# One set of order rules for the scheduler of an attention kernel, and small layer-norm steps moved to VectorE

## The chip, the cores and the metric

The kernel runs on one core of a Trainium2 chip. The metric is the device time of one execution in microseconds (us). Before the change it is 709.93 us, the median of three runs (709.76 to 710.06). The profiled execution shows a span of 708.0 us from the first to the last instruction.

## The reference, cut to what matters

A token block of 2048 rows and 640 columns is normalised; attention with 32 query heads of width 20 and one shared key and value head is added to a squared-ReLU feed-forward layer and to the input.

```python
xn = _layernorm(x)                                   # (x - mean) / sqrt(var + 1e-5)
q = (xn @ wq) -> 32 heads of 20;  k = xn @ wk;  v = xn @ wv
p = softmax((q @ k.T) * 20 ** -0.5)                  # 32 x 2048 x 2048
attention = (p @ v) -> (2048, 640) @ wo
h = relu(xn @ w1 + b1) ** 2                          # 2048 x 1536
return x + attention + (h @ w2 + b2)
```

The score matrix has 134 million elements. It is worked off in tiles of 128 keys by 512 queries: 4 query chunks x 8 groups of 4 heads make 32 blocks, and each block has 16 key tiles x 4 heads, so there are 2048 tiles in all. The four heads of one key tile are called a set when VectorE takes them.

## The kernel before

Two paths make the exponential of a score tile. ScalarE takes two or three tiles at a time from PSUM and writes exp to `PT`. VectorE and GpSimd take whole sets: VectorE turns each score into a 16-bit pattern whose bits, read as bf16, are a rough power of two; three more passes add a constant to the pattern (a quarter step each), on whichever of VectorE and GpSimd the scheduler expects to be done first; and four weighted value matmuls add the four approximations up.

```python
# a score step for ScalarE: 2 or 3 tiles, in as many PSUM banks
return Op(f"ACT{st_['j']}", "ACT", 0.05 + 0.4267 * n, [lambda e: e.activation(
    out=PT[:, s0:s0 + n, :], in_=ps[:, b0:b0 + (n - 1) * db + 1:db, :], func=AF.Exp, bias=-EXP_SHIFT, scale=SCALE)], deps)
# ... a tile for VectorE (tbuf lies in tmore or in x_sb)
d1 = op(f"D1_{n}_{i}", "DVE", 0.60, lambda e: e.tensor_scalar(
    out=L[:, cs].bitcast(U16), in0=ps[:, bank, :], scalar1=XA, scalar2=XB, op0=ALU.mult, op1=ALU.add), ...)
# ... and the three pattern passes of a full set
tp = max(free["POOL"] - now, 0.0) + sum(o.dur for o in pool_q) + 1.86
td = max(free["DVE"] - now, 0.0) + sum(o.dur for o in dve_q) + 0.6
eng = "POOL" if tp <= td + par("PBIAS") else "DVE"
```

TensorE makes the scores with four heads side by side on groups of 32 rows (one burst, called mode R in the code), and everything else (values, projections, feed-forward, output) in groups of four matmuls of 32 columns (mode C).

The order of the instructions on every engine is laid out before the launch by a list scheduler in the kernel's own Python. It keeps a clock for each engine, with durations written beside each operation, and always takes the ready operation that can start first; among those that could start within `EPS` the one with the lowest priority number. Some twenty parameters set those choices. They are read by `par`, and the kernel before overrides them anew for each stretch of 10 us of the scheduler's clock:

```python
STG = 10.0
RULES = {1: {'PVA': 0.95, 'EPS': 0.2, 'DGAP': 0.8},
         2: {'JIT': 0.9},
# ... some 55 rows cut
         69: {'R3': 0, 'WARM': 0.78, 'NOPEN': 1, 'URG': 2, 'D1P': 0.5, 'ND': 2, 'MPRIO': 0.9, 'DQP': 0.95, 'PBIAS': 1}}

def next_stage():
    while free["ACT"] >= stage[0] * STG:
        stage[0] += 1
        # ...
        now_rules.clear()
        now_rules.update(RULES.get(stage[0], {}))

def par(name):
    return now_rules.get(name, DEFAULTS[name])
```

A few of the parameters: `R3` sets how many PSUM banks must be free before three tiles rather than two go into one ScalarE step (at least 3 + R3); `NOPEN` is the number of VectorE sets that may be open at once; `DRATE` and `DLAST` decide until when a set is still taken from the current block; `PBIAS` favours GpSimd for a pattern pass; `MPRIO`, `PVA`, `DQP` are priorities of TensorE's work; `WARM` is the share of TensorE's time below which it puts in filler matmuls on zeros.

```python
banks = None
if len(ok) >= 3 + par("R3"):          # ok: banks that are free in time
    ap = [(a, a + d, a + 2 * d) for d in (1,) for a in range(NB - 2 * d) if {a, a + d, a + 2 * d} <= set(ok)]
    if ap:
        banks = list(ap[0])
if banks is None:
    can = sorted((max(st_of[bk], st_of[bk + 1], t0), bk) for bk in range(NB - 1) if ...)
    banks = [can[0][1], can[0][1] + 1]
```

Of the kernel before, what the change touches and what calls it, by code (L numbers as in the profile page):

```python
# [9 lines left out]
ALU = mybir.AluOpType  # L10
# [15 lines left out]
EPS = 1e-5  # L26
# [9 lines left out]
def _pl(z):  # L36
# [16 lines left out]
EVP = 0.8  # L53
JIT = 0.8
R3 = 2
NOPEN = 2
# [3 lines left out]
DRATE = 0.95  # L60
DLAST = 7.5
# [17 lines left out]
ACTEV = (0, 2)  # L79
KEEP = 1  # L80
DJIT = 9.0
RULES = {1: {'PVA': 0.95, 'EPS': 0.2, 'DGAP': 0.8},
         2: {'JIT': 0.9},
         3: {'JIT': 0.9, 'R3': 0},
         5: {'EPS': 0.2, 'DJIT': 0.6},
         6: {'SQP': 2, 'EPS': 0.06},
         7: {'SQP': 2, 'EPS': 0.06},
         8: {'DQP': 0.95, 'D1P': 1},
         9: {'MPRIO': 1.0},
         10: {'DRATE': 1.1, 'D1P': 1},  # L90
         12: {'R3': 2, 'ND': 1, 'JIT': 1.0, 'MPRIO': 1.1},
         13: {'NOPEN': 1, 'DRATE': 1.1},
         14: {'NOPEN': 1, 'DRATE': 1.1, 'KEEP': 2, 'DLAST': 3.5},
         15: {'R3': 1},
         16: {'R3': 1, 'DJIT': 1.0, 'ND': 3, 'DRATE': 0.8, 'DGAP': 0.25},
         17: {'R3': 1, 'DJIT': 1.0, 'ND': 3, 'DRATE': 0.8, 'DGAP': 0.25},
         18: {'PP': 0.9, 'NOPEN': 1},
         19: {'PP': 0.9, 'NOPEN': 1, 'EVP': 2, 'SQP': 1.5, 'DJIT': 9},
         20: {'PP': 4, 'NOPEN': 1, 'EVP': 2, 'SQP': 1.5, 'DJIT': 9},
         21: {'EVP': 2, 'URG': 2},  # L100
         22: {'JIT': 0.82},
         23: {'IDLE': 0.2, 'D1P': 3},
         24: {'IDLE': 0.2, 'D1P': 3, 'PBIAS': 1.5, 'DRATE': 0.95},
         25: {'DJIT': 0.6, 'DRATE': 0.95, 'URG': 4},
         26: {'D1P': 1, 'PVA': 2.1, 'DGAP': 0, 'DRATE': 0.95},
         27: {'JIT': 1.0, 'SQP': 0.7},
         28: {'EPS': 0.06, 'IDLE': 0.5},
         29: {'PP': 0.9, 'DRATE': 0.95, 'DLAST': 4.5},
         30: {'NOPEN': 3, 'DQP': 2.05, 'EPS': 0.12},
         38: {'DQP': 2.05, 'PBIAS': 2.5},  # L110
         39: {'DQP': 2.05, 'PBIAS': 2.5, 'PP': 2.5, 'IDLE': 0.1, 'ND': 1, 'DRATE': 1.1},
         40: {'DLAST': 2.5, 'R3': 1, 'EPS': 0.06, 'EVP': 0.3},
         41: {'DLAST': 2.5, 'R3': 1, 'EPS': 0.03, 'EVP': 0.3, 'DJIT': 0.3},
         42: {'DLAST': 2.5, 'R3': 1, 'EPS': 0.03, 'EVP': 0.3, 'DJIT': 0.3, 'PBIAS': 0.3},
         43: {'IDLE': 2, 'DJIT': 9, 'DLAST': 2.5, 'DRATE': 0.95},
         44: {'IDLE': 2, 'DJIT': 9, 'DLAST': 2.5, 'DRATE': 0.95, 'EPS': 0.12},
         45: {'IDLE': 2, 'DJIT': 9, 'DLAST': 2.5, 'DRATE': 0.95, 'EPS': 0.12, 'SQP': 0.7, 'BEHIND': -0.3, 'KEEP': 1},
         46: {'DGAP': 1.5, 'MPRIO': 1.1, 'BEHIND': 0.5},
         47: {'DGAP': 1.5, 'MPRIO': 0.5, 'BEHIND': 0.5, 'PBIAS': 0.3, 'R3': 1, 'NOPEN': 2},
         48: {'DGAP': 1.5, 'MPRIO': 0.5, 'BEHIND': 0.5, 'PBIAS': 0.3, 'R3': 1, 'NOPEN': 2, 'D1P': 0.5, 'DRATE': 1.1},  # L120
         49: {'DGAP': 1.5, 'MPRIO': 0.9, 'BEHIND': 0.5, 'PBIAS': 0.3, 'R3': 1, 'NOPEN': 2, 'D1P': 3, 'DRATE': 1.1, 'DLAST': 3.5, 'EVP': 2},
         50: {'DGAP': 1.5, 'MPRIO': 0.9, 'BEHIND': 0.5, 'PBIAS': 0.3, 'R3': 1, 'NOPEN': 2, 'D1P': 3, 'DRATE': 1.1, 'DLAST': 3.5, 'EVP': 2},
         51: {'DGAP': 1.5, 'MPRIO': 0.9, 'BEHIND': 0.5, 'PBIAS': 0.3, 'R3': 1, 'NOPEN': 2, 'D1P': 3, 'DRATE': 1.1, 'DLAST': 3.5, 'EVP': 2, 'EPS': 0.06, 'PP': 4},
         52: {'DGAP': 1.5, 'MPRIO': 0.9, 'BEHIND': 0.5, 'PBIAS': 2.5, 'R3': 1, 'NOPEN': 2, 'D1P': 1, 'DRATE': 1.1, 'DLAST': 3.5, 'EVP': 2, 'EPS': 0.06, 'PP': 4, 'SQP': 0.7, 'URG': 4},
         53: {'DGAP': 1.5, 'MPRIO': 0.9, 'BEHIND': 0.5, 'PBIAS': 2.5, 'R3': 1, 'NOPEN': 2, 'D1P': 1, 'DRATE': 1.1, 'DLAST': 3.5, 'EVP': 1.1, 'EPS': 0.06, 'PP': 2.5, 'SQP': 0.7, 'URG': 4},
         54: {'DGAP': 1.5, 'MPRIO': 0.9, 'BEHIND': 0.5, 'PBIAS': 2.5, 'R3': 1, 'NOPEN': 2, 'D1P': 1, 'DRATE': 1.1, 'DLAST': 3.5, 'EVP': 1.1, 'EPS': 0.06, 'PP': 2.5, 'SQP': 0.7, 'URG': 6, 'KEEP': 3},
         55: {'DGAP': 1.5, 'MPRIO': 0.9, 'BEHIND': 0.5, 'PBIAS': 2.5, 'R3': 1, 'NOPEN': 2, 'D1P': 1, 'DRATE': 1.1, 'DLAST': 3.5, 'EVP': 1.1, 'EPS': 0.06, 'PP': 2.5, 'SQP': 0.7, 'URG': 6, 'KEEP': 3},
         56: {'JIT': 0.82, 'MPRIO': 0.9, 'PP': 2.5},
         57: {'JIT': 0.82, 'MPRIO': 0.9, 'PP': 2.5, 'WARM': 0.85, 'R3': 1, 'SQP': 0.7},
         58: {'JIT': 0.82, 'MPRIO': 0.9, 'PP': 2.5, 'WARM': 0.85, 'R3': 1, 'SQP': 0.7},  # L130
         59: {'DLAST': 4.5},
         60: {'DLAST': 4.5, 'NOPEN': 2, 'MPRIO': 1.0},
         61: {'DLAST': 4.5, 'NOPEN': 2, 'MPRIO': 1.0},
         62: {'R3': 0, 'WARM': 0.78},
         63: {'R3': 0, 'WARM': 0.78, 'NOPEN': 1, 'URG': 2},
         64: {'R3': 0, 'WARM': 0.78, 'NOPEN': 1, 'URG': 2},
         65: {'R3': 0, 'WARM': 0.78, 'NOPEN': 1, 'URG': 2},
         66: {'R3': 0, 'WARM': 0.78, 'NOPEN': 1, 'URG': 2, 'D1P': 1, 'ND': 2, 'MPRIO': 0.9, 'DQP': 0.95},
         67: {'R3': 9, 'WARM': 0.78, 'NOPEN': 1, 'URG': 2, 'D1P': 1, 'ND': 2, 'MPRIO': 0.9, 'DQP': 0.95},
         68: {'R3': 9, 'WARM': 0.78, 'NOPEN': 1, 'URG': 2, 'D1P': 0.5, 'ND': 2, 'MPRIO': 0.9, 'DQP': 0.95, 'PBIAS': 1},  # L140
         69: {'R3': 0, 'WARM': 0.78, 'NOPEN': 1, 'URG': 2, 'D1P': 0.5, 'ND': 2, 'MPRIO': 0.9, 'DQP': 0.95, 'PBIAS': 1}}
HOOK = None
PRIO = {'XN1': 0.13}
NBEF = {'S4a': 6.0, 'AG5': 10.23, 'PW1': 4.94}
# [90 lines left out]
def bass_parallel_sum__grouped_kv_mqa__dense_activation_squared_relu__prompt_kernel(nc, A_x, A_wq, A_wk, A_wv, A_wo, B_x, B_w1, B_b1, B_w2, B_b2, out):  # L235
    es = ExitStack()
    with es:
# [118 lines left out]
        def op(name, eng, dur, fn, deps=(), **kw):  # L356
            o = Op(name, eng, dur, [fn], deps, **kw)
            o.prio = PRIO.get(name, o.prio)
            o.nb = NBEF.get(name, 0.0)
            ev = [d for d in o.deps if isinstance(d, str)]  # L360
            if ev:
                late.setdefault(ev[0], []).append(o)
            else:
                QUE[eng].append(o)
            return o
# [59 lines left out]
        def rows(st):  # L425

            p = ROWP[st // 4]
            small, pp = (("DVE", 0.08), p - 0.1) if st < 4 else (("POOL", 0.13), st // 4 - 0.5)
            if st in ACTST:
                k = ACTST.index(st)  # L430
                jk = OC[:, 0, :, :].rearrange("p c n -> p (c n)")[:, k * D:(k + 1) * D] if k < 4 else out_sb[:, k - 4, :]
                s1 = op(f"S{st}a", "ACT", 0.72, lambda e: e.activation(out=jk, in_=x_sb[:, st, :], func=AF.Identity, scale=-1.0 / D, accum_out=mv[:, st, 0:1]), [x_op[st]], lat=0.2)
                ag = op(f"S{st}b", "ACT", 0.9, lambda e: e.activation(out=jk, in_=x_sb[:, st, :], func=AF.Square, bias=mv[:, st, 0:1], accum_out=mv[:, st, 1:2]), [s1], lat=0.25)
                ve = op(f"VE{st}", "DVE", 0.08, lambda e: e.tensor_scalar(out=mv[:, st, 1:2], in0=mv[:, st, 1:2], scalar1=1.0 / D, scalar2=EPS, op0=ALU.mult, op1=ALU.add), [ag], prio=p - 0.1)
                opm = ALU.add
            else:
                s1 = op(f"S{st}a", "DVE", 0.40, lambda e: e.bn_stats(out=stats6[:, st, 0, :], in_=x_sb[:, st, 0:320]), [x_op[st]], prio=p)  # L437
                s2 = op(f"S{st}b", "DVE", 0.40, lambda e: e.bn_stats(out=stats6[:, st, 1, :], in_=x_sb[:, st, 320:640]), [x_op[st]], prio=p)  # L438
                ag = op(f"AG{st}", "DVE", 0.19, lambda e: e.bn_aggr(out=mv[:, st, :], in_=stats6[:, st, :, :].rearrange("p a b -> p (a b)")), [s1, s2], prio=p - 0.1)
                ve = op(f"VE{st}", *small, lambda e: e.tensor_scalar(out=mv[:, st, 1:2], in0=mv[:, st, 1:2], scalar1=EPS, scalar2=None, op0=ALU.add), [ag], prio=pp)  # L440
                opm = ALU.subtract
                if st in POOLXN:
                    s1 = op(f"NM{st}", *small, lambda e: e.tensor_scalar(out=mv[:, st, 0:1], in0=mv[:, st, 0:1], scalar1=-1.0, scalar2=None, op0=ALU.mult), [ag], prio=pp)
                    opm = ALU.add
            pw = op(f"PW{st}", "POOL", 0.52, lambda e: e.tensor_tensor(out=rstd[:, st:st + 1], in0=mv[:, st, 1:2], in1=nhalf[:, 0:1], op=ALU.pow), [ve, c_half], lock=True, prio=st // 4)  # L445
            eng, dur = ("POOL", 0.87) if st in POOLXN else ("DVE", 0.36)
# [579 lines left out]
        def new_set():  # L1026
            b = cur["b"]
            now = free["PE"]
            opn = sum(1 for s in sets[-NL:] if s["left"])
            back = max(free["POOL"] - now, 0.0) + sum(o.dur for o in pool_q) + opn * 1.5 * 1.86  # L1030
            need = max(back, HPG * par("DRATE") * (1 + opn)) + par("DLAST")
            if len(unclaimed[b]) * HPG * 0.4523 * 0.85 + DSLACK <= need:
                b += 1
# [438 lines left out]
```

The softmax here doesn't subtract the row's maximum and nothing guards it: scores larger than these inputs give would overflow.

## Time and profile before

| what | us | share of the span |
|---|---|---|
| device time, median of 3 | 709.93 | |
| span of the profiled execution | 708.0 | |
| TensorE weight loads busy | 218.5 | 31% |
| VectorE busy | 634.3 | 90% |
| ScalarE busy | 691.3 | 98% |
| GpSimd busy | 442.0 | 62% |
| first exponential starts | 13.7 | |
| last exponential ends | 699.0 | |

A group in the profile is one line of the kernel, one engine, one operation and one pair of tiles. Its columns are the count, the busy time in us, the mean duration of one in ns, and the idle time of the engine just before it with what ended that idle time. L921 is ScalarE's exponential, L1096 VectorE's pattern from a score tile, L1114 the pattern pass (on either engine), and L377 the line of a helper through which almost all matmuls go, so that they are told apart by their tiles: `qT,kT` are scores, `PT,vx` values of ScalarE's tiles, `tmore,vx`, `tmore,vxs` and `x_sb,vxs` values of VectorE's sets. L440 and L443 are the small layer-norm operations that the change moves. The granted TensorE clock is full in every slice.

### The profile page before, as it was taken

The numbers are of one execution on the slowest core, as the hardware profiler recorded it, in microseconds if no ns is written. First come the engines' busy times: TensorE is split into PE (matmuls) and PEld (weight loads), VectorE is DVE, ScalarE is ACT, GpSimd is POOL, SyncE is SP. The second block draws the span as 40 slices with busy tenths as digits, with TensorE's granted clock in tenths as the row PEclk, the third lists the DMA queues.
The fourth block names the chain that finished last, engine by engine and source line by source line (L and its number), as shares of the span: only waits on it lengthen the run. The fifth ranks groups of instructions, "written<-read, shape, count | busy, mean of one in ns | idle before, by whom it ended". The sixth has DMA issues, their size and how long they took to land.

```text
span 708.0 us, 22589 instructions
## 1 busy us (share of the span) xinstructions
PE 697.3 (98%) x9787; PEld 218.5 (31%) x9788; DVE 634.3 (90%) x1090; ACT 691.3 (98%) x741; POOL 442.0 (62%) x291
## 2 busy tenths in 40 slices
PE   8999999999999999999999999999999999999997
PEld 4432223223322223322333222233333322233333
DVE  7769999999999999999999899889999889997693
ACT  7799999999999999999999999999999999999995
POOL 3856785587578755566567755647577787635353
PEclk9999999999999999999999999999999999999999
DMA  6316422323137700111111101012111100132201
GB/s 203 113 40 156 122 57 67 92 91 87 55 75 177 179 15 21 46 38 48 50 32 39 24 17 28 22 35 54 36 52 29 48 18 16 26 100 55 59 25 40
DMA packets 42016, 44.01 MB, mean 62 GB/s; under 512 B 15540, under 2 KB 32772, under 8 KB 41788
## 3 DMA queue, kind: packets, MB, share of 16 engines
q1 hardware_dynamic: 39132, 36.93, 19.0%
q0 software_dynamic: 2208, 5.25, 3.6%
q8 instruction: 77, 1.26, 0.7%
q10 hardware_dynamic: 576, 0.38, 0.2%
q14 instruction: 23, 0.19, 0.1%
HBM read 28.03 MB, written 14.91 MB: 61 GB/s over the span
## 4 chain that ended last, share of the span: by engine, by line
ACT 89%; PE 7%; DVE 1%; POOL 1%; DMA 0%; issue 0%; DVEq 0%
ACT PT L921 89%; PE ps L377 6%; DMA x_sb<-in_A_x_dram 0%; PE ps L551 0%; POOL rstd L445 0%; DVE big L447 0%; PE ps L579 0%; DVE OR L438 0%; DVE xnT L554 0%; DVE out_sb L1177 0%; DVE OR L437 0%; PE ps L521 0%; PE ps L486 0%; POOL big L447 0%; PE ps L507 0%
## 5 line engine op out<-in xcount | busy, mean ns | idle before, releaser
L921 ACT ACTIVATE PT<-ps 128x1024 bf16<-128x1024 f32 (+1 forms) x719 | 681.2, 1214 | 5.5 <-PE ps L377 5.2
L1096 DVE TENSOR_SCALAR tmore<-ps 128x512 uint16<-128x512 f32 x560 | 362.6, 683 | 37.7 <-PE ps L377 33.0
L1114 POOL TENSOR_SCALAR tmore<-tmore 128x2048 uint16<-128x2048 uint16 x107 | 202.3, 1898 | 151.8 <-DVE tmore L1114 40.9
L377 PE MATMUL ps<-qT,kT 20*128 20x512 bf16 x2048 | 283.4, 384 | 2.5 <-ACT PT L921 1.7
L1114 POOL TENSOR_SCALAR x_sb<-tmore 128x2048 uint16<-128x2048 uint16 x108 | 203.8, 1897 | 89.0 <-DVE x_sb L1114 41.5
L377 PEld LDWEIGHTS ps<-qT,kT 20*128 20x128 bf16 x2048 | 72.1, 91 | 278.9 <-ACT PT L921 237.0
L377 PE MATMUL ps<-PT,vx 128*32 128x512 bf16 x1488 | 139.3, 386 | 0.9 <-ACT PT L921 0.6
L1114 DVE TENSOR_SCALAR x_sb<-tmore 128x2048 uint16<-128x2048 uint16 x124 | 87.3, 732 | 0.0
L377 PE MATMUL ps<-x_sb,vxs 128*32 128x512 bf16 x928 | 82.5, 382 | 0.0
L377 PE MATMUL ps<-xnT,w_sb 128*32 128x512 bf16 x960 | 77.0, 384 | 0.0
L377 PE MATMUL ps<-w_sb,big 128*32 128x320 bf16 x1536 | 74.8, 302 | 0.2 <-DVE tmore L1096 0.2
L377 PE MATMUL ps<-tmore,vxs 128*32 128x512 bf16 x752 | 68.4, 382 | 0.0
L1114 DVE TENSOR_SCALAR tmore<-tmore 128x2048 uint16<-128x2048 uint16 x81 | 60.8, 773 | 0.1
L377 PEld LDWEIGHTS ps<-PT,vx 128*32 128x32 bf16 x1488 | 35.8, 94 | 65.7 <-issue 55.6
L377 PE MATMUL ps<-tmore,vx 128*32 128x512 bf16 x560 | 54.9, 382 | 0.0
L377 PEld LDWEIGHTS ps<-w_sb,big 128*32 128x32 bf16 x1536 | 32.6, 95 | 29.2 <-issue 19.9
L659 DVE TENSOR_SCALAR hT_tmp<-ps,b1col 128x512 bf16<-128x512 f32 x48 | 35.7, 744 | 6.1 <-PE ps L377 5.1
L377 PE MATMUL ps<-xnT,wq_sb 128*32 128x512 bf16 (+1 forms) x480 | 33.9, 356 | 0.0
L377 PE MATMUL ps<-wo_c,OC 128*32 128x320 bf16 x608 | 32.1, 302 | 0.0
L377 PEld LDWEIGHTS ps<-x_sb,vxs 128*32 128x32 bf16 x928 | 21.4, 95 | 19.4 <-issue 13.2
L377 PEld LDWEIGHTS ps<-xnT,w_sb 128*32 128x32 bf16 x960 | 18.2, 94 | 27.2 <-issue 21.9
L377 PEld LDWEIGHTS ps<-tmore,vxs 128*32 128x32 bf16 x752 | 17.7, 95 | 15.9 <-issue 12.7
(83 smaller groups left out, 266.7 us busy)
## 6 DMA issues: line engine op xcount, KB each, us to landing
xbd<-b2d SPq DMA_DIRECT2D x16, 320.0 KB, 4.4
xbd<-in_A_x_dram POOLq DMA_DIRECT2D x8, 640.0 KB, 7.3
xr<-xbd SPq DMA_DIRECT2D x32, 160.0 KB, 2.4
w_sb<-in_B_w_dram SPq DMA_DIRECT2D x8, 480.0 KB, 4.3
big<-OR SPq DMA_DIRECT2D x71, 40.0 KB
big<-drs SPq DMA_DIRECT2D x71, 40.0 KB
out_dram<-out_sb SPq DMA_DIRECT2D x15, 160.0 KB, 1.9
qT<-QCr SPq DMA_DIRECT2D x108, 20.0 KB
```

The lines of the kernel that those rows point to most:

```text
L377: return lambda e: e.matmul(out_, l, r, start=start, stop=stop, tile_position=tp)
L659: o = Op(f"RL{qc}_{f}", "DVE", 0.66, [lambda e: e.tensor_scalar(out=hT_tmp[:, k % 2, :], in0=ps[:, bk, :], scalar1=b1col[:, f:f + 1], scal ...
L921: return Op(f"ACT{st_['j']}", "ACT", 0.05 + 0.4267 * n, [lambda e: e.activation(out=PT[:, s0:s0 + n, :], in_=ps[:, b0:b0 + (n - 1) * db + ...
L1096: d1 = op(f"D1_{n}_{i}", "DVE", 0.60, lambda e: e.tensor_scalar(out=L[:, cs].bitcast(U16), in0=ps[:, bank, :], scalar1=XA, scalar2=XB, op0 ...
L1114: p = op(f"P{j}_{n}", eng, 0.60 if eng == "DVE" else 1.86, lambda e, T=T, j=j, two=two: e.tensor_scalar(out=T.bitcast(U16), in0=L.bitcast( ...
```

## The change

It has three parts. The first concerns the moment at which VectorE's next set is opened: the scheduler compares what is left in the block with GpSimd's backlog, and the backlog no longer counts GpSimd's work that is not a pattern pass (only those carry a block number, `blk`), so that a set isn't pushed to the next block by a layer norm or a transfer in GpSimd's queue. The second makes the epsilon and the negated mean of row tiles 4 to 15 on VectorE, where those of tiles 0 to 3 are made already, in place of GpSimd. The third takes the table of rules by stage away: the default values of the parameters hold for the whole span, which makes the kernel's order a matter of one set of rules.

```diff
-RULES = {1: {'PVA': 0.95, 'EPS': 0.2, 'DGAP': 0.8},
-         2: {'JIT': 0.9},
 ... (the rest of the table cut)
-         69: {'R3': 0, 'WARM': 0.78, 'NOPEN': 1, 'URG': 2, ..., 'PBIAS': 1}}
+RULES = {}
@@ rows(st)
-            small, pp = (("DVE", 0.08), p - 0.1) if st < 4 else (("POOL", 0.13), st // 4 - 0.5)
@@
-                ve = op(f"VE{st}", *small, lambda e: e.tensor_scalar(out=mv[:, st, 1:2], ..., scalar1=EPS, ...), [ag], prio=pp)
+                ve = op(f"VE{st}", "DVE", 0.08, lambda e: e.tensor_scalar(out=mv[:, st, 1:2], ..., scalar1=EPS, ...), [ag], prio=p - 0.1)
@@
-                    s1 = op(f"NM{st}", *small, lambda e: e.tensor_scalar(out=mv[:, st, 0:1], ..., scalar1=-1.0, ...), [ag], prio=pp)
+                    s1 = op(f"NM{st}", "DVE", 0.08, lambda e: e.tensor_scalar(out=mv[:, st, 0:1], ..., scalar1=-1.0, ...), [ag], prio=p - 0.1)
@@ new_set()
-            back = max(free["POOL"] - now, 0.0) + sum(o.dur for o in pool_q) + opn * 1.5 * 1.86
+            back = max(free["POOL"] - now, 0.0) + sum(o.dur for o in pool_q if o.blk is not None) + opn * 1.5 * 1.86
```

More of the change, by code (lines that the diff above doesn't have):

```diff
@@ L81 @@
 DJIT = 9.0
-RULES = {1: {'PVA': 0.95, 'EPS': 0.2, 'DGAP': 0.8},
-         2: {'JIT': 0.9},
[L84 to L141, printed above, removed]
@@ L439, in rows @@
                 ag = op(f"AG{st}", "DVE", 0.19, lambda e: e.bn_aggr(out=mv[:, st, :], in_=stats6[:, st, :, :].rearrange("p a b -> p (a b)")), [s1, s2], prio=p - 0.1)
-                ve = op(f"VE{st}", *small, lambda e: e.tensor_scalar(out=mv[:, st, 1:2], in0=mv[:, st, 1:2], scalar1=EPS, scalar2=None, op0=ALU.add), [ag], prio=pp)
+                ve = op(f"VE{st}", "DVE", 0.08, lambda e: e.tensor_scalar(out=mv[:, st, 1:2], in0=mv[:, st, 1:2], scalar1=EPS, scalar2=None, op0=ALU.add), [ag], prio=p - 0.1)
                 opm = ALU.subtract
                 if st in POOLXN:
-                    s1 = op(f"NM{st}", *small, lambda e: e.tensor_scalar(out=mv[:, st, 0:1], in0=mv[:, st, 0:1], scalar1=-1.0, scalar2=None, op0=ALU.mult), [ag], prio=pp)
+                    s1 = op(f"NM{st}", "DVE", 0.08, lambda e: e.tensor_scalar(out=mv[:, st, 0:1], in0=mv[:, st, 0:1], scalar1=-1.0, scalar2=None, op0=ALU.mult), [ag], prio=p - 0.1)
                     opm = ALU.add
```

## The prediction, made before the change was run

> **What bounds the kernel now.** I read the page's busy line first, then the chain of waits, the windows of steady state, the groups by form and one microsecond of the timeline.
>
> ```profile
> PE 697.3 (98%) x9787; PEld 218.5 (31%) x9788; DVE 634.3 (90%) x1090; ACT 691.3 (98%) x741; POOL 442.0 (62%) x291
> ```
>
> Two engines stand at 98%. The chain in order of time says which one ended last:
>
> ```profile
> 39.73 223.16 ACT PT L921 x241
> 262.94 24.73 PE ps L377 x359
> 287.69 409.98 ACT PT L921 x428
> 697.72 4.32 PE ps L377 x116
> ```
>
> From 39.73 to 697.72 us it is ScalarE's exponentials, with one stretch where TensorE ended last: they are near a tie. The windows, whose columns are busy us of PE, PEld, DVE, ACT and POOL:
>
> ```profile
> 100.00:200.00 100.00, 99.40 (x1406) 30.53 (x1402) 95.05 (x158) 100.00 (x108) 64.61 (x35) 1.00 0.26 74
> 300.00:400.00 100.00, 99.87 (x1410) 30.38 (x1408) 95.26 (x157) 100.00 (x109) 63.86 (x35) 1.00 0.15 40
> ```
>
> ScalarE has no idle microsecond, VectorE has 5%, and GpSimd has a third of its time free. The groups by form give the work:
>
> ```profile
> L921 ACT ACTIVATE PT<-ps 128x1024 bf16<-128x1024 f32 x669 | 625.9, 1184 | 3.4 <-PE ps L377 3.2
> L921 ACT ACTIVATE PT<-ps 128x1536 bf16<-128x1536 f32 x50 | 79.4, 1622 | 2.1 <-PE ps L377 2.1
> L1096 DVE TENSOR_SCALAR tmore<-ps 128x512 uint16<-128x512 f32 x560 | 362.6, 683 | 37.7 <-PE ps L377 33.0
> ```
>
> Of 2048 score tiles ScalarE takes 669 x 2 + 50 x 3 = 1488, VectorE 560. The mean durations overlap (an activation is not over when the next starts); the distance between starts, read one by one in the trace, has a median of 904 ns for two tiles and 1330 ns for three. Three tiles in one instruction save 0.5 x 904 x 3 - 1330 = 26 ns, little. What TensorE pays is seen in the timeline:
>
> ```profile
> 302.61 0.39 PE L377 MATMUL ps<-qT,kT 20*128 20x512 bf16 x3
> 302.93 0.40 PE L377 MATMUL ps<-x_sb,vxs 128*32 128x512 bf16 x4
> 303.15 0.39 PE L377 MATMUL ps<-xnT,wq_sb 128*32 128x512 bf16 x4
> 303.47 0.42 PE L377 MATMUL ps<-qT,kT 20*128 20x512 bf16 x3
> ```
>
> Starts tell more than durations here. Two groups of four 32-column matmuls start 0.22 us apart (302.93 to 303.15); a group and a score burst 0.32 us (303.15 to 303.47), and a score burst and a group 0.32 us (302.61 to 302.93). So a burst costs 0.215 + 2 x 0.10 = 0.42 us, and it costs that whether two, three or four heads ride in it. Groups of 320 columns start 0.137 us apart. Counting every instruction at its cost, TensorE has about 680 us of work and ScalarE's exponentials 671 + some 9 of small waits (12 ns each): neither can take more work without lengthening the kernel.
>
> [...]
>
> **The change, part by part.** All three parts act through the kernel's own list scheduler, which lays out every engine's order before the launch. I therefore compared the orders that result, and counted.
>
> Part 1, the title's: the estimate of GpSimd's backlog counts only pattern passes. Made alone on the kernel before, the order of all five queues stays the same, instruction by instruction; made on the kernel without stage rules it also changes nothing. Where score sets are opened, GpSimd's queue holds nothing else that tips the comparison. Its share: 0.0 us.
>
> Part 2: epsilon and negated mean for tiles 4 to 15 go from GpSimd to VectorE: 18 instructions, 11 + 7. On GpSimd they take 226 and 221 ns (so 4.0 us busy), on VectorE 154 ns (2.8 us), all within the first 35 us. GpSimd is 8.8 of 10 us busy from 20 to 30 us, VectorE 8.6. I expect the saving of the one and the load of the other to cancel to within 1 us at the start. Made alone, with the stage rules kept, this part makes the rules act on another state than they were made for: VectorE gets 532 tiles and ScalarE 1516.
>
> Part 3: the table of order rules for 10 us stages goes. This changes nearly every row of the order. The totals of the kernel changed, against before:
>
> - score tiles on VectorE 556 (560); on ScalarE 1492 (1488)
> - activations of two tiles 722 (669), of three 16 (50): 738 in all (719)
> - score bursts of TensorE between other work 730 (713)
> - filler groups, [...] 13 (10); patterns multiplied per set 139 x 4 (140 x 4)
> - pattern passes on VectorE 201 (205), on GpSimd 216 (215)
>
> ScalarE: 722 x 0.904 + 16 x 1.330 = 674.0, before 669 x 0.904 + 50 x 1.330 = 671.3. It pays +2.7 us.
> TensorE: 17 bursts x 0.42 = 7.2; two more activation steps that share a burst, 2 x 0.215 = 0.4; three fillers x 0.22 = 0.7; one set less, 4 groups x 0.22 = -0.9, and one more group of ScalarE tiles +0.2; a warm-up matmul 0.3. Sum +7.9 us.
> VectorE: 18 x 0.154 - 4 x 0.65 (362.6 / 560 of its row) - 4 x 0.72 (148.1 us for 205 passes, the sum of its two rows) = -2.7 us. It is relieved.
>
> The two 98% engines must not be added. I cut both orders into 16 stretches of 93 ScalarE tiles and took for each stretch the larger of TensorE's and ScalarE's work. Before: ScalarE 41.8 to 43.1, TensorE 40.1 to 42.4 in all but the first stretch (54.7, TensorE) and the end (6.8, TensorE): sum 698.4. After: TensorE is over ScalarE in stretch 7 (43.4 to 42.6) and 12 (43.7 to 42.6), the first stretch has 55.8, and the end, after ScalarE's first 1488 tiles, has 11.1 (+4.3): sum 707.4, so +9.0. With stretches of 8 tiles, the most that the seven banks let one engine run ahead, 704.2 becomes 711.5: +7.3; with 186 tiles +6.6. The first of these leaves 710 - 704 = 6 us for what isn't in it (launch, first load, the last output), and so stands near the measured time without any fitting. I take +8.
>
> The end itself: once VectorE has turned the last block, TensorE before has 16 groups of 0.137 us left; after has 28, since only four of the eight output halves, not six, were begun. 12 x 0.137 = 1.6 us; it is part of the +4.3.
>
> On top I put 1 us for stalls that counting can't see: without rules for each stage the queues meet less well. The filler groups stand for such places, 5 of the 13 close together past the middle, where TensorE had nothing ready. 709.9 + 8 + 1 = 719.
>
> **Rivals.** (a) VectorE is the hidden limit, and its relief pays: for this speaks its 95% and 33 us in which it waited for TensorE, against it that ScalarE waited for nobody in steady state. It would give 2 to 4 us back: 714 to 716. (b) Orders that look balanced by count stall in practice: the engines run in order, and a burst that waits for VectorE's release of a bank holds the next activation. For it: TensorE's weight loads waited 245 us in total for ScalarE in 613 short pieces, so the coupling is tight; against it: the order before has the same coupling and only 5.2 us of ScalarE idling. If stalls of 0.02 us per activation came in, 738 x 0.02 = 15 us: 733. (c) The head becomes quicker, since GpSimd loses about a fifth of its work from 16 to 33 us, where its small operations run back to back between the reciprocal roots: up to 2 us. Against it: TensorE is busy 10.0 of 10 us right behind, from 30 to 40 us.
>
> **Range and chances.** The work added is fixed by the counted order, so faster by over 2% (below 695.7) would need ScalarE to run through 674 us of exponentials with fewer waits than a kernel that has hardly any: 1%. Slower by over 2% starts at 724.1, 5 us over my value; rival (b) at a third of its size gets there: 13%. The rest, 86%, is within 2%. My range for 8 in 10 is 714.5 to 725: the lower end is rival (a) with (c), the upper the stage sum of +9 with 6 us of stalls.
>
> **What would show it.** The trace of the kernel changed should have 738 activations whose starts lie 904 and 1330 ns apart at the median; ScalarE's last exponential should end near 706 (699 before) and some 11 us should follow it (9 before). TensorE's windows should stay near 99 of 100. If ScalarE's idle time before PT is well over 10 us in steady state, rival (b) holds; if the last exponential ends before 702, the addition of TensorE's bursts was wrong, and TensorE had slack that the distances of starts did not show. If the first 93 tiles end later or earlier by over 2 us, part 2 was mis-sized.

## The result and the profile after

The changed kernel takes 719.19 us (median of 3 runs, 718.53 to 721.15) against 709.93 us: a ratio of 1.0137 with a 95% interval of 1.0106 to 1.0168. The prediction was 719.0. First the busy line of the page, then the chain of waits in order of time (start, length, engine, what), both of the kernel changed:

```profile
PE 705.8 (98%) x9787; PEld 219.6 (31%) x9789; DVE 642.5 (90%) x1100; ACT 694.1 (97%) x760; POOL 439.3 (61%) x274
```

```profile
39.97 243.76 ACT PT L861 x263
...
334.12 16.12 ACT PT L861 x17
...
354.95 165.05 ACT PT L861 x179
520.04 31.68 PE ps L318 x451
551.73 10.96 PE ps L318 x134
...
565.64 83.04 ACT PT L861 x90
...
666.41 42.65 PE ps L318 x688
```

The chain was almost all ScalarE before; now TensorE carries long pieces of it, from 284 to 334, from 520 to 564 and from 666 us on. Such pieces show the near tie and not what it costs: in the run with a table made anew, below, TensorE has 30% of the chain, and that kernel takes 708.78 us. TensorE gained 8.5 us of busy time, ScalarE 2.8. The groups by form, the exponentials of two and of three tiles, and VectorE's patterns:

```profile
L861 ACT ACTIVATE PT<-ps 128x1024 bf16<-128x1024 f32 x722 | 666.9, 1185 | 7.5 <-PE ps L318 7.3
L861 ACT ACTIVATE PT<-ps 128x1536 bf16<-128x1536 f32 x16 | 25.5, 1593 | 1.0 <-PE ps L318 1.0
L1036 DVE TENSOR_SCALAR tmore<-ps 128x512 uint16<-128x512 f32 x556 | 358.8, 682 | 36.6 <-PE ps L318 33.1
```

Read by starts, two tiles take 904 ns and three 1330 ns at the median, as before. The span splits along ScalarE: until the first exponential, the exponentials at those two figures, all else up to the end of the last, and what follows it.

| | first starts | exponentials | waits and rest | after the last | span |
|---|---|---|---|---|---|
| before | 13.7 | 671.3 | 14.0 | 9.0 | 708.0 |
| after | 14.6 | 674.0 | 16.8 | 11.3 | 716.7 |

The 8.7 us are 0.8 + 2.7 + 2.8 + 2.3, each rounded. Where they arise shows when the trace is cut at every 93rd tile of ScalarE (at the start of the activation that takes it), as the prediction cut the order: stretch 7 takes 44.4 us (42.6 before; they are counted from 0), stretch 12 takes 44.9 (42.5), and from tile 1488 to the end it is 14.9 (10.7). The other stretches lie within 0.7 us of before, save the first two: stretch 0 ends 0.8 us earlier and stretch 1 takes 1.1 us longer, since their border falls on another activation. Windows of the kernel changed over stretches 7, 12 and, beside them, 8 (columns as in the prediction):

```profile
315.10:359.50 44.40, 44.27 (x678) 14.71 (x669) 39.28 (x65) 42.88 (x48) 20.22 (x12) 1.00 0.19 52
530.20:575.10 44.90, 44.79 (x627) 13.59 (x619) 39.83 (x66) 42.76 (x47) 30.37 (x17) 1.00 0.14 35
359.50:401.90 42.40, 42.40 (x535) 11.55 (x531) 40.78 (x67) 42.40 (x48) 24.08 (x13) 1.00 0.10 25
```

In stretches 7 and 12 TensorE is busy throughout and ScalarE is short by 1.5 and 2.1 us. Each time it is one wait. This is the first, in the timeline of the kernel changed (other rows left out):

```profile
331.96 0.39 PE L318 MATMUL ps<-qT,kT 20*128 20x512 bf16 x3
...
333.26 0.59 PE L318 MATMUL ps<-wo_c,OC 128*32 128x320 bf16 x12
333.68 1.04 PE L318 MATMUL ps<-PT,vx 128*32 128x512 bf16 x16
...
334.12 3.28 ACT L861 ACTIVATE PT<-ps 128x1024 bf16<-128x1024 f32 x3 [1.39 <-PE ps L318]
```

The scores of the waiting exponential were made at 331.96, long in time. What it waits for is a free place in `PT`, a ring of 20 tiles: the value matmuls that empty it, the first of a new block, come at 333.68, four groups in one go, behind the output matmuls. They could have gone from 330.02 on, when VectorE had copied the old block's sums: both blocks add up in the same PSUM bank, so the copy must come first. The second wait:

```profile
562.64 0.49 PE L318 MATMUL ps<-qT,kT 20*128 20x512 bf16 x4
563.06 0.61 PE L318 MATMUL ps<-x_sb,vxs 128*32 128x512 bf16 x8
...
563.97 0.68 DVE L929 COPY OR<-ps 128x512 f32<-128x512 f32 x1
...
565.20 1.04 PE L318 MATMUL ps<-PT,vx 128*32 128x512 bf16 x16
565.64 1.94 ACT L861 ACTIVATE PT<-ps 128x1024 bf16<-128x1024 f32 x2 [2.15 <-PE ps L318]
```

Here the new block's values follow the copy's end (564.65) by 0.55 us. What is late is the end of the old block: its last two value groups go at 563.06, though the pattern passes that they read were over at 560.77. They stand behind scores and feed-forward matmuls.

### The profile page after: what moved, and what is told of

Its sections match the earlier page's. It is cut to its first block, busy times and chain, and to the rows that moved or that the text cites. A ratio compares the mean times of both kernels' runs of the same rounds, so it can differ in the third digit from the quotient of the medians.

```text
span 716.7 us, 22623 instructions
## 1 busy us (share of the span) xinstructions
PE 705.8 (98%) x9787; PEld 219.6 (31%) x9789; DVE 642.5 (90%) x1100; ACT 694.1 (97%) x760; POOL 439.3 (61%) x274
## 4 chain that ended last, share of the span: by engine, by line
ACT 71%; PE 25%; DVE 2%; DMA 1%; issue 0%; SPq 0%
ACT PT L861 71%; PE ps L318 24%; DVE tmore L1036 1%; DMA x_sb<-in_A_x_dram 1%; PE ps L491 1%; DVE tmore L1054 0%; PE ps L519 0%; DVE x_sb L1054 0%; PE ps L447 0%; ACT OC L372 0%; SPq L335 0%; DVE OC L955 0%; PE ps L426 0%; SPq L342 0%; ACT xnT L428 0%
## 5 line engine op out<-in xcount | busy, mean ns | idle before, releaser
L1036 DVE TENSOR_SCALAR tmore<-ps 128x512 uint16<-128x512 f32 x556 | 358.8, 682 | 36.6 <-PE ps L318 33.1
L1054 POOL TENSOR_SCALAR tmore<-tmore 128x2048 uint16<-128x2048 uint16 x115 | 217.1, 1896 | 154.3 <-PE ps L318 57.3
L318 PE MATMUL ps<-qT,kT 20*128 20x512 bf16 x2048 | 291.3, 384 | 4.4 <-ACT PT L861 3.0
L1054 POOL TENSOR_SCALAR x_sb<-tmore 128x2048 uint16<-128x2048 uint16 x101 | 190.6, 1896 | 88.7 <-DVE x_sb L1054 34.2
L318 PEld LDWEIGHTS ps<-qT,kT 20*128 20x128 bf16 x2048 | 74.3, 91 | 289.7 <-ACT PT L861 239.3
L1054 DVE TENSOR_SCALAR x_sb<-tmore 128x2048 uint16<-128x2048 uint16 x129 | 98.8, 794 | 0.5 <-PE ps L318 0.5
L318 PE MATMUL ps<-w_sb,big 128*32 128x320 bf16 x1536 | 77.3, 302 | 0.3 <-DVE tmore L1036 0.3
L1054 DVE TENSOR_SCALAR tmore<-tmore 128x2048 uint16<-128x2048 uint16 x72 | 53.1, 750 | 0.2 <-PE ps L318 0.2
L607 DVE TENSOR_TENSOR big<-hT_tmp 128x512 bf16<-128x512 bf16 x48 | 27.0, 573 | 0.2
L318 PEld LDWEIGHTS ps<-xnT,w_sb 128*32 128x32 bf16 x960 | 17.8, 94 | 28.0 <-issue 22.5
```

The costliest lines, as they stand in the source:

```text
L318: return lambda e: e.matmul(out_, l, r, start=start, stop=stop, tile_position=tp)
L607: q = op(f"SQ{qc}_{f}", "DVE", 0.34, lambda e: e.tensor_tensor(out=h2T[:, f, :], in0=hT_tmp[:, k % 2, :], in1=hT_tmp[:, k % 2, :], op=ALU. ...
L1054: p = op(f"P{j}_{n}", eng, 0.60 if eng == "DVE" else 1.86, lambda e, T=T, j=j, two=two: e.tensor_scalar(out=T.bitcast(U16), in0=L.bitcast( ...
```

## The experiments

Two questions: which part of the change costs what, and why ScalarE waits in just those places. Theory 1 is the prediction's counting: time follows the sum, over stretches, of the larger of TensorE's and ScalarE's work in the order laid out. Theory 2 is the rival that parts and rules have effects of their own, which add up.

**The parts alone.** The first run undoes everything but the empty table.

```diff
-RULES = {1: {...}, ... 69: {...}}      # of the kernel before; nothing else changed
+RULES = {}
```

> The table of stage rules is removed, alone; the small layer-norm steps stay on GpSimd. Theory 1 (count the order: for each stretch the larger of TensorE's and ScalarE's work): with stretches of 8 tiles the sum is 717.0 against 704.2 of before, with 93 tiles 712.0 against 698.4, so 722.5 to 723.5 us. Theory 2 (each part has an effect of its own and they add up; the small steps are worth at most 1 us): as the whole change, 718 to 720 us.

Measured: 723.58 us, 1.0193 [1.0165, 1.0222]. Theory 1 had it, within 0.1 us: without its second part the change is dearer. The profiled execution, the slowest of four (727.20 us at a mean clock of 0.991, with the clock at 0.50 for 13.7 us from 645.8 on), had 17.8 us after the last exponential, 9.0 before: output work had piled up at the end.

The second run leaves the table and moves the small operations:

```diff
-                ve = op(f"VE{st}", *small, ..., prio=pp)
+                ve = op(f"VE{st}", "DVE", 0.08, ..., prio=p - 0.1)     # and NM{st} likewise
```

> Only the epsilon and negated mean are moved to VectorE; the stage rules stay. Theory 1 (counting): ScalarE gets 1516 tiles, sum 713.4 (stretches of 93) to 725.1 (of 8) against 698.4 and 704.2, so 725 to 731 us, slower than the whole change. Theory 2 (own effects that add up): 709 to 711 us.

Measured: 728.91 us, 1.0255 [1.0227, 1.0283]; this is the median of three (mean clocks 0.992 to 1.000); a fourth execution took 753.47 us at a mean clock of 0.955. Theory 1 had it. Eighteen operations of 0.15 us, all in the first 31 us, cost 18 us, twice the whole change. It isn't their work: the first 93 tiles of ScalarE end at 61.0 us (60.2 before), and ScalarE gets 28 tiles more. The table was made for another state.

The third run adds the backlog rule to the second:

```diff
-            back = ... + sum(o.dur for o in pool_q) + opn * 1.5 * 1.86
+            back = ... + sum(o.dur for o in pool_q if o.blk is not None) + opn * 1.5 * 1.86
```

> The small steps on VectorE and the backlog that counts pattern passes alone; the stage rules stay. Here the backlog rule does alter the order (it alters nothing in the kernel before). Theory 1 (counting): sum 710.9 to 721.3 against 698.4 and 704.2, so 722 to 727 us, some 3 us under the run without the backlog rule. Theory 2 (own effects that add up, the backlog 0): the same as the run without it, 709 to 711 us.

Measured: 734.13 us, 1.0361 [1.0296, 1.0425]. Both theories missed: it isn't 3 us faster than the second run but, by the medians, 5.2 slower. Part of that is the clock: the two slowest of the four executions (738.00 and 739.83) had mean clocks of 0.986 and 0.981. At full clock it is 729.39 against 726.25, 3.1 slower. The timeline of this run shows what the counting leaves out:

```profile
660.75 0.39 PE L377 MATMUL ps<-tmore,vxs 128*32 128x512 bf16 x4
...
661.38 0.68 DVE L988 COPY OR<-ps 128x512 f32<-128x512 f32 x1
...
662.12 0.83 PE L377 MATMUL ps<-PT,vx 128*32 128x512 bf16 x12 [0.21 <-DVE OR L988]
662.57 1.45 ACT L920 ACTIVATE PT<-ps 128x1536 bf16<-128x1536 f32 x1 [3.29 <-PE ps L377]
```

The block's last value group (660.75, a set of VectorE's) is followed by the copy of the sums (661.38), the copy by the new block's first value matmuls (662.12), and only they free a place for ScalarE, which had waited for 3.29 us. A block that closes late fills the ring, whatever the sums of work say. The run has two waits over 2.5 us of ScalarE, at 264 and 663 us; the second run has one, at 443. That at 264 is within a block: a value group whose last tile was ready at 253.7 goes at 263.2, behind other values and projections.

The four corners tell the most. Taking the table away costs 13 us where the small operations are on GpSimd, the state that it was made for (710.49 to 723.58). Where they are on VectorE, with the backlog rule, it gains 15 us (734.13 to 719.19; 11 at full clock). So the parts have no effects of their own that could be added.

Then one single rule in the kernel changed:

```diff
-RULES = {}
+RULES = {30: {'MPRIO': 1.1}}
```

> The kernel changed with a single rule in a single stretch of 10 us (from 290 to 300 us of the scheduler's clock the priority number of a begun unit is 1.1, behind the value matmuls, in place of 0.9). Theory 1 (counting): one small turn re-deals everything after it: sum 715.0 (8 tiles) and 710.4 (93) against 711.5 and 707.4, so +3.0 to +3.5, 722 to 723 us. Theory 2 (a rule acts where it stands): within 0.5 us of the kernel changed, 719 us.

Measured: 720.67 us, 1.0164 [1.0126, 1.0202]. By time it can't be told from the kernel changed, and theory 1 put it 1.3 to 2.3 us too high. By the trace, theory 2 falls: ScalarE's waits at 334 and 565 us, 40 and 270 us behind the rule, are gone; there is a new one of 1.72 us at 692; the last exponential ends at 704.0 (705.4), and 15.0 us follow it (11.3). One small turn re-deals everything behind it.

**Doses on the kernel before.** 100 groups on zeros for TensorE:

```diff
+        # every ninth value group of a block already begun
+                    o.parts = fill_parts() + o.parts
```

> The kernel before, with its order, and 100 groups of four matmuls on zeros (0.22 us each, 22 us of TensorE work) put evenly in front of every ninth value matmul. Theory 1 (TensorE and ScalarE near a tie, about 1.2 us of TensorE slack per stretch of 93 tiles): +4.6 (stretches of 93) to +11 us (of 8), so 714.5 to 721 us. Rival: TensorE's 98% comes from modelled ends and it has room: 710 us. Second rival: TensorE alone is the limit: +22, 732 us.

Measured: 721.88 us, 1.0160 [1.0146, 1.0173], so 11.6 of the 22 us show. Neither rival holds: TensorE is neither free nor alone. The figure lies just over theory 1's range, at the side of the short stretches. And 47 tiny exponentials for ScalarE:

```diff
+        # every fifteenth exponential
+                    o.parts = [lambda e: e.activation(out=scr[:, 3:4], in_=scr[:, 0:1], func=AF.Exp)] + o.parts
```

> The kernel before, with its order, and 47 extra exponentials of one column on ScalarE, one ahead of every fifteenth. If one costs about 0.2 us between starts (the single one at the start of the kernel takes 203 ns), ScalarE gets 9 to 10 us. Theory 1: ScalarE is the larger in 15 of 16 stretches, so nearly all of it shows: 718 to 720 us. Rival (VectorE and GpSimd set the pace, or TensorE alone): 710 to 712 us.

Measured: 714.21 us, 1.0055 [1.0041, 1.0069]. My size for one was wrong; the group of this run reads

```profile
L1389 ACT ACTIVATE scr<-scr 128x1 f32<-128x1 f32 x47 | 16.4, 350 | 1.7 <-PE ps L377 1.7
```

One lasts 350 ns, but with one in between, the starts of two exponentials lie 996 ns apart instead of 904: it takes 92 ns of ScalarE. 47 x 0.092 = 4.3 us, and 3.9 came out in the time (4.3 in the span). So ScalarE's work shows almost wholly, TensorE's by half: ScalarE is the first bound, and TensorE has some 10 us in hand (22 less 11.6, an estimate), spread over the span.

**Without fillers.**

```diff
+        for o in seq["PE"]:
+            if o.name == "fill" and len(o.parts) == 4:
+                o.parts = []
```

> The kernel changed, without the 13 groups of filler matmuls in steady state (2.9 us of TensorE work); its order is otherwise the same. Theory 1: they stand where TensorE had nothing to do, and the stretches they lie in are ScalarE's: the sum is the same, 719 us, within 0.7. Rival: they keep the clock up, and without them it drops below 1.00: above 720 us. Second rival: TensorE's work sets the time: 716.3 us.

Measured: 722.16 us, 1.0170 [1.0156, 1.0184]: 3 us slower for 2.9 us less work (2.3 by the ratios). The rival is right: the mean clock is 0.991 to 0.993 in all five executions. Windows of this run where fillers had stood (the figure behind POOL's count is the granted TensorE clock):

```profile
440.00:442.00 2.00, 1.65 (x26) 0.52 (x22) 1.87 (x4) 2.00 (x4) 1.62 (x1) 1.00 0.21 67
442.00:444.00 2.00, 1.43 (x15) 0.39 (x12) 2.00 (x4) 2.00 (x3) 2.00 (x2) 1.00 0.15 32
...
446.00:448.00 2.00, 2.00 (x24) 0.70 (x26) 1.50 (x3) 1.41 (x3) 1.70 (x1) 0.50 0.17 41
448.00:450.00 2.00, 2.00 (x27) 0.72 (x23) 0.30 (x1) 1.30 (x2) 2.00 (x2) 0.50 0.00 0
...
452.00:454.00 2.00, 2.00 (x30) 0.47 (x32) 1.94 (x4) 1.81 (x3) 0.00 (x0) 1.00 0.27 62
```

TensorE pauses for 0.92 us in 4 us, no single pause over 0.4, and from 444.56 its clock is at 0.50 for 6.83 us (0.64 over the window from 444 to 446, 0.65 over that from 450 to 452). Over 446 to 450 us ScalarE gets only 2.7 us of work out of 4. Start by start, ScalarE loses 2.3 us here against the kernel changed, 0.6 us at 248 and 1.3 us at 118, where the clock is 0.92 over the window from 100 to 120 us, against 1.00 in the kernel changed (the end gives 0.7 back). The run below with the turn mended has 0.94 over the same window with every filler in place, so that part is not shown to be theirs.

**The two waits.** What makes them: is it the amount of TensorE's work in the stretch (1a), or that the value matmuls on which a new block hangs stand too far behind (1b)? First the turn, with the amount unchanged:

```diff
+        for name, of in [("PV14_0", "OUT5.3"), ("PV14_1", "OUT5.7"), ("PV14_2", "OUT5.10"), ("PV14_3", "OUT5.14")]:
+            ahead(name, of)       # the value group goes in front of that output group
```

> The kernel changed, with four groups of value matmuls of block 14 (the first that read the ScalarE tiles of a new block) moved ahead of some output matmuls in the same 3 us near 331 us; TensorE's work stays the same. Theory 1a (amount: TensorE has 43.4 us of work in the stretch against ScalarE's 42.6): the wait of ScalarE of 1.39 us at 334 us stays or moves by a few us, and the time with it: 719 us. Theory 1b (turn of the block: ScalarE's ring of 20 tiles is full, since the value matmuls that empty it stand behind output matmuls): the wait is gone, below 0.2 us, 717.8 us.

Measured: 719.15 us, 1.0125 [1.0111, 1.0139], no gain. ScalarE in the timeline of this run:

```profile
335.53 1.02 ACT L861 ACTIVATE PT<-ps 128x1024 bf16<-128x1024 f32 x1 [0.17 <-PE ps L318]
...
337.25 5.18 ACT L861 ACTIVATE PT<-ps 128x1536 bf16<-128x1536 f32 x5 [0.69 <-PE ps L318]
```

The wait has come apart. But from 320 to 340 us the starts of the exponentials are late by 1.62 us in sum over their medians, against 1.80 without the move: with TensorE busy for 24.96 of the 25 us from 320 to 345, the value groups moved ahead hold up the scores instead. That speaks for 1a. Then less work, the order unchanged; the kernel leaves out part of the output and projections, so its output isn't the reference's:

```diff
+        gone = {f"OUT{n}.{k}" for n in (4, 5) for k in range(3, 11)} | {f"{u}.{k}" for u in ("QC3_3", "FFN2_0", "FFN2_1") for k in (1, 2, 3)}
+        # the matmuls of the groups in gone are not issued
```

> The kernel changed, with its order, but with TensorE work left out just ahead of ScalarE's two long waits: 16 groups of output matmuls before 334 us (2.2 us) and 9 groups of projection matmuls before 565 us (2.0 us). Theory 1a (amount: the waits of 1.39 and 2.15 us are TensorE's surplus in these stretches): both waits fall below 0.3 us and the time by 3 to 3.5 us, to 715.7 to 716.2. Theory 1b (a turn of the block that comes late for another reason, such as a pattern pass or the copy of the sums): at least one of them stays, and the time falls by under 2 us, above 717.

Measured: 723.20 us, 1.0177 [1.0158, 1.0197]. Less work, and 4 us slower. It settles nothing about the waits, for TensorE fell idle and its clock with it: from 325 to 330 us it is busy for 3.81 of 5 us, from 330 to 335 its clock is at 0.50, and over the five executions the mean clock is 0.986 to 0.993. The last run takes out less, and never two groups in a row:

```diff
+        gone = {f"OUT4.{k}" for k in (2, 5, 8, 11, 14)} | {f"OUT5.{k}" for k in (1, 4, 7, 10, 13)} | {"QC3_3.2", "FFN2_0.1", "FFN2_0.3", "FFN2_1.1", "FFN2_1.3"}
```

> As the run with work left out, but less and spread: 10 groups of output matmuls before 334 us (1.4 us), never two in a row, and 5 groups of projection matmuls before 565 us (1.1 us), so that TensorE is never idle for long and its clock stays at 1.00. Theory 1a (amount): the wait at 334 us falls from 1.39 to below 0.4 and that at 565 us from 2.15 to about 1.1, the time by 1.8 to 2.4 us to 716.8 to 717.4. Theory 1b (turn): the waits stay within 0.3 us of 1.39 and 2.15, the time at 719.

Measured: 719.55 us (717.47 to 724.21), 1.0125 [1.0104, 1.0147]; the times scatter with the clock (a mean of 0.991 in the slowest of the four, 1.000 in the two fastest). The profiled execution is the slowest, but at both places its clock was 1.00. The waits are 1.23 us (at 341, later in this run) and 1.96 us: as good as unchanged, as 1b expects. The timeline of this run says how:

```profile
336.11 0.69 DVE L929 COPY OR<-ps 128x512 f32<-128x512 f32 x1 [0.21 <-PE ps L318]
...
339.64 0.39 PE L318 MATMUL ps<-qT,kT 20*128 20x512 bf16 x2
339.96 0.59 PE L318 MATMUL ps<-wo_c,OC 128*32 128x320 bf16 x12
340.38 1.04 PE L318 MATMUL ps<-PT,vx 128*32 128x512 bf16 x16
...
340.82 1.02 ACT L861 ACTIVATE PT<-ps 128x1024 bf16<-128x1024 f32 x1 [1.23 <-PE ps L318]
```

The old block's sums are copied at 336.80, and the value groups could go. They go at 340.38, because four bursts of scores, with outputs between them, stand before them in TensorE's order, each of which waits for ScalarE to give back a bank. Time won by TensorE is lost at those bursts: it is idle for 0.85 us from 330 to 340. So at 334, with the old order the turn binds, and with the turn mended the amount binds; either alone leaves 1.6 us or more of the 1.8. For 565 only the amount was tried. Both mended at once was not tried, and the times leave room for the amount: the two executions of this run at full clock took 717.47 and 718.37 us, the two of the kernel changed 718.53 and 719.19. That is some 1 us less, of which the traced waits show 0.35.

**Other rules.** One set of rules still, with other values:

```diff
+DEFAULTS.update(EVP=2, IDLE=0.1, D1P=3, WARM=0.6, DRATE=0.9, SQP=1.5, PVA=0.95, DGAP=1.5)
```

> The kernel changed, still with one set of rules for the whole span, but other values for eight parameters (among them value matmuls before units less often tied, and no fillers). Theory 1 (counting): sum 707.7 (stretches of 8) and 703.6 (93) against 711.5 and 707.4 of the kernel changed, so 3.8 us under it: 714 to 716 us. Rival (default values or others are the same, it is the stages that matter): 719 us. If TensorE's clock drops for want of fillers, up to 3 us more.

Measured: 713.01 us, 1.0036 [1.0024, 1.0048]: 6 us better than the kernel changed, at equal parts 2 and 3, and 1 us under theory 1's range. It has no filler groups, and its clock stays at 1.00 in all five executions. And a table made anew for this state (it begins with stage 4 and has 19 rows), on top of those eight values:

```diff
+RULES = {4: {'R3': 1},
+         11: {'PVA': 2.1},
+         15: {'PVD': 2.1},
+         ...
+DEFAULTS.update(EVP=2, IDLE=0.1, D1P=3, WARM=0.6, DRATE=0.9, SQP=1.5, PVA=0.95, DGAP=1.5)
```

> The kernel changed with a table of stage rules again, but one made for this state (small steps on VectorE, the backlog rule). Theory 1 (counting): sum 703.2 (8) and 698.2 (93), against 704.2 and 698.4 of before: 709 to 711 us, level with the kernel before. Rival (the small steps on VectorE cost by themselves; with rules kept they cost 16 us): 716 us or more.

Measured: 708.78 us, 0.9985 [0.9974, 0.9997], just under the kernel before. Its busy line and the exponentials:

```profile
PE 699.6 (99%) x9761; PEld 216.2 (31%) x9761; DVE 644.0 (91%) x1119; ACT 690.0 (98%) x751; POOL 430.1 (61%) x269
```

```profile
L881 ACT ACTIVATE PT<-ps 128x1024 bf16<-128x1024 f32 x703 | 651.2, 1181 | 4.8 <-PE ps L338 4.7
L881 ACT ACTIVATE PT<-ps 128x1536 bf16<-128x1536 f32 x26 | 41.3, 1587 | 0.8 <-PE ps L338 0.8
```

703 x 0.904 + 26 x 1.330 = 670.1 us of exponentials, 4 less than in the kernel changed, and 8.6 us after the last. Of the 10.4 us that it is under the kernel changed, the eight values give 6.2 and the table 4.2. The small operations on VectorE cost nothing when the order is made for them.

All counted sums (stretches of 8 tiles) beside the medians:

| kernel | counted | measured | difference |
|---|---|---|---|
| rules anew | 703.2 | 708.78 | 5.6 |
| before | 704.2 | 709.93 | 5.7 |
| other values | 707.7 | 713.01 | 5.3 |
| changed | 711.5 | 719.19 | 7.7 |
| one rule | 715.0 | 720.67 | 5.7 |
| rules removed alone | 717.0 | 723.58 | 6.6 |
| small and backlog | 721.3 | 734.13 | 12.8 |
| small alone | 725.1 | 728.91 | 3.8 |

## Why the prediction was right

- **Part 1 is 0.0.** The program built is the same with and without it, in the kernel before and in the kernel changed; there is nothing to measure. Beyond that the claim doesn't reach: with the small operations moved and the old table kept, the backlog rule does re-deal the order, and the run with it was slower.
- **Part 2 within 1 us at the start.** The activation with the 93rd tile starts at 59.4 us, 0.8 earlier than before. Rival (c), a head quicker by up to 2 us, is worth no more than that. But the second run shows that the place of these operations matters through the order it brings about, and by far more than their work.
- **The sums.** ScalarE +2.7 by count and +2.8 in its busy time. The trace has 730 score bursts between other work, against 713, as counted. TensorE's +7.9 stands beside +8.5 of busy time, but that is no test: in the run with 100 groups on zeros, 22 us of added work raise it by 14.1 (697.3 to 711.4). The activations number 738, the last ends at 705.4 (predicted 706), and 11.3 us follow it (11).
- **The stretches.** 7 and 12 were named, at 43.4 and 43.7; they took 44.4 and 44.9. The end was to grow by 4.3 and grew by 4.2. That the total came out within 0.2 us owes something to luck. The +8 was picked between sums of +6.6 and +9.0. The 1 us that was put on top for stalls stands for 1.0 and 1.2 us in just these two stretches, and the first stretch, counted 1.1 us longer, came out 0.8 us shorter (0.1 longer by the next start).
- **The cause of these two waits was half right.** The prediction said that TensorE has too much work there. That is one of two conditions; the other is the turn of the values behind scores and other matmuls. For the wait at 334 the runs show both, for that at 565 the turn is read from the order and not tested.
- **VectorE was mis-sized.** Its busy time was to fall by 2.7 us and rose by 8.2 (634.3 to 642.5). The moved operations take 0.143 to 0.145 us, near the 0.154 that was assumed, but its passes into `x_sb` went from a mean of 732 to 794 ns and the squares from 464 to 573 ns. What made them longer stays open. The relief that rival (a) needs did not come, so the kernel changed doesn't test it; but the run with a table made anew has VectorE busy for 644.0 us, 9.7 more than before, and is no slower, so that load does not set the time.
- **Rival (b), stalls in practice,** is at work in the run with small operations and backlog: at full clock it lies 2.4 us over theory 1's range, and by the median 7, the rest of which comes with lower clocks. In the kernel changed the waits grew by under 3 us.

## What to carry to other kernels

When two engines are near a tie, count each one's work by stretches and sum the larger; it placed seven of eight orders within 3.9 us of each other's offset, though two of them differ by 20 us. A table of values found for one order can cost more than none in another (11 to 15 us here): re-make it after every change of the state it was made for, and don't judge a small change by a run with the old table. And look where a ring is emptied: the instruction that frees a place must not stand, in an in-order queue, behind ones that wait for the engine which needs that place: in the run with less left out, value groups in such a turn went at 340.38, 3.58 us after the copy that they had waited for.

## What the runs showed of the hardware that I had not expected

In the run without fillers TensorE's clock fell to 0.50 after pauses that were short and few: 0.92 us in the 4 us from 440 to 444, none over 0.4 us, and then 6.83 us at half. The run with 25 groups of work left out shows half clock behind idle time in two places: TensorE is busy for 3.81 of the 5 us from 325 to 330, at a clock of 0.79, and the clock is at 0.50 from 330 to 335; it is busy for 3.69 of the 5 us from 560 to 565, at 0.84, and the clock is at 0.50 from 565 to 570. How much idle time it takes is not shown. With this the run was 4 us slower than the kernel changed, though it has less work. The 13 groups on zeros, put where TensorE would be idle, save 2 to 3 us. The last two runs under "Other rules" have no such groups, and their mean clock is at 1.00 in 18 of 19 executions.

In the run with 47 tiny exponentials one lasts 350 ns and takes 92 ns of ScalarE, from one start of its neighbours to the next (996 ns against 904): the duration in the profile is not what it costs.
